# Row loads of two token blocks moved to GpSimd's queue in a fused attention and ReGLU training step

## The chip, the cores and the metric

The kernel runs on one core of a Trainium2 chip. A core has five engines that each work through their own list of instructions in order: TensorE (PE) for matrix products, VectorE (DVE), ScalarE (ACT), GpSimd (POOL) and SyncE (SP), which issues most data transfers. Transfers are issued into queues and carried out by the core's 16 DMA engines. The metric is the time of one execution on the device, in microseconds (us).

## The reference

A forward pass and its gradients by all weights and by `x`, in bf16. For 2048 tokens of width 512, a gate `g` mixes sliding-window attention (32 heads of 16, window 256) with a gated ReGLU feed-forward layer of 1376 columns:

```
x = A_x                                           # 2048 x 512
g = sigmoid((x * gate_w).sum(-1, keepdims=True))
q, k, v = heads(x @ wqkv)                         # 32 heads, 16 wide
scores = q k^T * 16**-0.5, kept where 0 <= i - j < 256
a = concat(softmax(scores) v) @ wo
gate = x @ W_gate; up = x @ W_up                  # 2048 x 1376
b = (gate * (gate > 0) * up) @ W_down
out = g * a + (1 - g) * b
grads = vjp(out)(grad_out)   # for x, wqkv, wo, W_gate, W_up, W_down, gate_w
```

There are eight outputs: `out` and seven gradients, out_7 being that of `gate_w` (512 values).

## The kernel before, in words

All work is written as small operations, each with the engines that may do it, an estimated duration, a rank, and the buffers it reads and writes. A planner (`Flow.run`) then plays through time when the kernel is built: at each moment it gives every idle engine the ready operation of lowest rank, and writes its instructions into that engine's list. So the order on each engine is fixed when the kernel runs, and comes from ranks, estimated durations and 27 seeds (`SEEDS`) that spread the ranks of dense products. An engine waits in order: an instruction that waits holds up all behind it.

SBUF is one big tile, `arena`, cut by hand into rings of buffers (`ring`), which may lie on top of one another where one group is used only after another. PSUM is eight banks that are handed out under caps by name (`CAP_S` for scores, `CAP_DP` and so on).

The stages overlap freely:

- Rows. `x` and `grad_out` are kept in SBUF as rows (`x_r`, `db_r`), in four blocks of 512 tokens. `load_first` (L726, L731) brings block 0 and the first weights through SP's and ACT's queues; `load_rows` (L717) brings blocks 1 to 3 through SP's queue, 512 KB each. `rows_to_T` (L772) turns each block on PE into `x_T` and `db_T`. The rows of `grad_out` are first scaled by 1 - g on DVE (L847), after `gates` has computed the gate of that block (L833 on PE, L839 to L841 on ACT).
- Projections. `proj` (through L673) makes q, k, v and the gradient on the heads for four chunks of 128 columns and stores them to DRAM (L808), from where the attention loads them again (L977 to L979). The weights of chunk 1 and of the first two feed-forward chunks come by POOL's queue (L699, L710); `proj_weights` regroups weights on POOL (L814, L817) and stores them (L820).
- Attention. 32 stages; in each, PE computes scores and their gradients (L1049), ACT the exponentials (L1090), POOL the mask (L1066), DVE a product (L1096), and PE the sums over keys or queries (L1112). The kinds of products are called row, col and den (dense) in the planner, which counts a cost for a switch between them.
- Feed-forward. `front` makes three products for each block and three elementwise products (L902, by DVE or POOL) and stores them (L905); `back` makes the weight gradients.
- The end. `early` makes the feed-forward part of tokens (L1401 on PE), `dw` the gradients of wqkv and wo (dWqkv rows are evicted into `dwst` and stored at L1329, dWo at L1337), and `final` and `whole` finish each token block: for twelve of the sixteen, two partial results (`b_d`, `dx_p`) are loaded again (L1489, L1490), POOL adds them (L1508, L1514), and SP stores the sums (L1510, L1516). `gate_sum` adds up `gate_w`'s gradient over the token blocks in a long sum on DVE (L1469), which is turned into two bf16 parts (L1472, L1473); `direct` (L1480) adds these parts and the last three token blocks by five small products, and the result is stored at L1563.

Where PE has nothing ready, the planner puts a dummy product into its list (L1568). A few lines of the constants and the loads:

```
gw_b = mc.tile([P, D], BF, name="gw_b")
gw_rep = mc.tile([P, DC, P], BF, name="gw_rep")
...
for sb in range(1, NSB):
    load_rows(x_r, x_d, sb)
    load_rows(db_r, go_d, sb)
```

## Time and profile before

| what | value |
|---|---|
| median of 3 runs | 814.55 us (811.65 to 815.1) |
| the profiled execution's own time | 811.5 us |
| its span, first to last instruction | 809.8 us |
| busy: PE, DVE, ACT, POOL | 785.8, 703.5, 595.6, 540.2 us |
| granted TensorE clock, mean | 1.000 |
| data moved | 152.18 MB, mean 188 GB/s |

The span is the part of the execution that the trace covers; 1.7 us lie around it. "Busy" of PE counts pipelined products, whose ends are modelled. Each instruction is named by the line of the kernel that wrote it; L673 and L1401 are helpers through which dense products of several stages pass, L651 and L653 the copies out of PSUM by ACT and DVE.

### The profile page before, as it was taken

To read this page: it belongs to the slowest core of one execution; us is meant where nothing else is said; L and a number is where in the kernel's file an instruction comes from. 1 tells how busy PE (TensorE), PEld (TensorE's weight loads), DVE (VectorE), ACT (ScalarE), POOL (GpSimd) and SP (SyncE) were. 2 spreads that over 40 slices of the span, in tenths; PEclk is the share of its full clock that TensorE was granted. 3 is DMA by queue.
4 is the path that set the end of the run, shared out by engine and by line. 5 is a ranking of instruction groups with operands and counts; after the bars stand their busy time and mean duration, and the time that the engine had idled before them with its cause. 6 is when DMAs were issued, how large, how long until landed. Compare 5 with 4: busy or idle time off the path is not lost.

```text
span 809.8 us, 24095 instructions
## 1 busy us (share of the span) xinstructions
PE 785.8 (97%) x8845; PEld 371.4 (46%) x8950; DVE 703.5 (87%) x1273; ACT 595.6 (74%) x1183; POOL 540.2 (67%) x950
## 2 busy tenths in 40 slices
PE   8899999999999999999999999999999999999998
PEld 5534444544445445454554545444434344344443
DVE  3589999999998999999999989999999999934664
ACT  4776988898888888888888887889888878413221
POOL 2488678787796979969888765666656666212235
PEclk9999999999999999999999999999999999999999
DMA  8699457577499997988998895963765547797996
GB/s 229 186 205 228 126 137 172 118 177 177 118 204 169 227 181 227 209 170 242 200 186 186 236 219 148 191 184 103 201 158 175 145 141 177 228 267 204 267 206 196
DMA packets 313009, 152.18 MB, mean 188 GB/s; under 512 B 203161, under 2 KB 303194, under 8 KB 312250
## 3 DMA queue, kind: packets, MB, share of 16 engines
q1 hardware_dynamic: 294706, 136.47, 70.3%
q10 hardware_dynamic: 17688, 12.72, 5.6%
q0 software_dynamic: 496, 1.44, 0.8%
q8 instruction: 70, 1.15, 0.6%
q14 instruction: 49, 0.40, 0.2%
HBM read 55.02 MB, written 55.74 MB: 137 GB/s over the span
## 4 chain that ended last, share of the span: by engine, by line
PE 81%; DVE 8%; issue 3%; DMA 3%; ACT 3%; POOL 1%; SPq 0%; POOLq 0%; DVEq 0%; ACTq 0%
PE banks L673 36%; PE banks L1401 18%; PE banks L1049 15%; PE banks L1112 9%; DVE arena L1096 3%; ACT arena L1090 2%; DMA arena<-b_d 1%; PE banks L772 1%; DVE arena L902 1%; PE banks L1147 1%; DMA out_dram<-arena 1%; DVE arena L897 1%; DMA arena<-HD_d 1%; DMA arena<-in_A_x_dram 0%; DVE arena L1145 0%
## 5 line engine op out<-in xcount | busy, mean ns | idle before, releaser
L1096 DVE TENSOR_TENSOR arena<-arena,banks 128x512 bf16<-128x512 bf16 (+1 forms) x740 | 456.2, 665 | 21.9 <-PE banks L1049 15.6
L1066 POOL TENSOR_SCALAR_AFFINE_SELECT arena<-arena 128x256 bf16<-128x256 bf16 (+1 forms) x752 | 354.3, 494 | 166.1 <-ACT arena L1090 145.4
L1090 ACT ACTIVATE arena<-banks 128x512 bf16<-128x512 f32 (+1 forms) x740 | 396.9, 588 | 87.1 <-PE banks L1049 68.0
L673 PE MATMUL banks<-arena 128*128 128x512 bf16 (+4 forms) x1915 | 382.9, 334 | 5.8 <-issue 2.6
L673 PEld LDWEIGHTS <-arena 128*128 128x128 bf16 (+1 forms) x1984 | 173.6, 98 | 154.7 <-issue 56.4
L1401 PE MATMUL banks<-arena 128*128 128x512 bf16 (+1 forms) x749 | 182.6, 380 | 3.4 <-issue 2.4
L1049 PE MATMUL banks<-arena 32*128 32x128 bf16 (+5 forms) x2944 | 157.2, 270 | 4.2 <-DVE arena L1096 1.8
L1049 PEld LDWEIGHTS <-arena 32*128 32x128 bf16 (+1 forms) x2944 | 48.8, 92 | 141.1 <-issue 137.9
L1401 PEld LDWEIGHTS <-arena 128*128 128x128 bf16 (+1 forms) x784 | 69.5, 98 | 89.6 <-issue 18.4
L902 POOL TENSOR_TENSOR arena<-arena 128x512 bf16<-128x512 bf16 (+1 forms) x84 | 97.9, 1169 | 16.0 <-DVE arena L897 15.0
L1112 PE MATMUL banks<-arena 128*32 128x128 bf16 (+5 forms) x2944 | 94.5, 271 | 1.0 <-DVE arena L1096 0.5
L651 ACT CAST arena<-banks 128x512 bf16<-128x512 f32 (+4 forms) x158 | 77.6, 502 | 22.8 <-PE banks L673 17.6
L1112 PEld LDWEIGHTS <-arena 128*32 128x32 bf16 (+1 forms) x2944 | 60.7, 95 | 32.4 <-issue 16.2
L1508 POOL TENSOR_TENSOR arena<-arena 128x512 bf16<-128x512 f32 x12 | 15.5, 1292 | 47.7 <-DMA arena<-b_d 25.5
L1143 POOL TENSOR_TENSOR arena<-arena 128x512 bf16<-128x512 f32 x32 | 37.0, 1155 | 9.4 <-issue 5.7
L1507 ACT ACTIVATE arena<-banks,g_all 128x512 f32<-128x512 f32 x12 | 8.0, 684 | 45.1 <-DVE arena L1498 16.5
L902 DVE TENSOR_TENSOR arena<-arena 128x512 bf16<-128x512 bf16 (+1 forms) x48 | 35.8, 752 | 0.2
L1514 POOL TENSOR_TENSOR arena<-arena 128x512 bf16<-128x512 f32 x12 | 16.1, 1341 | 21.5 <-DVE arena L1512 13.2
L897 DVE SCALAR_TENSOR_TENSOR arena<-arena,banks 128x512 bf16<-128x512 bf16 (+1 forms) x44 | 29.9, 679 | 0.2
L892 ACT ACTIVATE arena<-banks 128x512 bf16<-128x512 f32 (+1 forms) x41 | 25.0, 610 | 2.0 <-PE banks L673 1.5
L653 DVE CAST arena<-banks 128x512 bf16<-128x512 f32 (+2 forms) x42 | 23.8, 580 | 2.1 <-PE banks L673 0.9
L1498 DVE SCALAR_TENSOR_TENSOR arena<-banks,g_all,arena 128x512 bf16<-128x512 f32 x12 | 9.0, 746 | 18.2 <-ACT arena L1507 15.5
(96 smaller groups left out, 414.1 us busy)
## 6 DMA issues: line engine op xcount, KB each, us to landing
ffn_d<-arena SPq DMA_DIRECT2D x40, 384.0 KB
arena<-ffn_d SPq DMA_DIRECT2D x88, 128.0 KB
out_dram<-arena SPq DMA_DIRECT2D x66, 128.0 KB
arena<-HD_d ACTq DMA_DIRECT2D x26, 256.0 KB
KV_d<-arena SPq DMA_DIRECT2D x32, 128.0 KB
QD_d<-arena SPq DMA_DIRECT2D x32, 128.0 KB
arena<-KV_d SPq DMA_DIRECT2D x32, 128.0 KB
arena<-QD_d SPq DMA_DIRECT2D x32, 128.0 KB
```

Of the source, the lines that this page charges most:

```text
L651: nc.scalar.copy(out, in_)
L673: return lambda start, stop: nc.tensor.matmul(out_fn(), lhsT=lhs_fn(), rhs=rhs_fn(), start=start, stop=stop)
L892: nc.scalar.activation(q["rg"][:fs, :], gps[:fs, :], ACT.Relu)
L897: op({DVE: t_stt(W)}, lambda e, q=q, ups=ups: nc.vector.scalar_tensor_tensor(out=q["upm"][:fs, :], in0=q["rg"][:fs, :], scalar=0.0, in1=up ...
L902: op({POOL: t_pool(W, 2), DVE: DTT}, lambda e, q=q, k=k, a=a, b=b: EN[e].tensor_tensor(out=q["act"][:fs, k, :], in0=q[a][:fs, :], in1=q[b] ...
L1049: nc.tensor.matmul(bank, lhsT=lt[rs, ls], rhs=rt[rs, rsl], start=True, stop=True)
L1066: nc.gpsimd.affine_select(out=v.rearrange("p h (b k) -> p h b k", b=cnt), in_=v.rearrange("p h (b k) -> p h b k", b=cnt), compare_op=ALU.i ...
L1090: op({ACTE: t_act(w)}, lambda e, h=h: nc.scalar.activation(nxt.Pt[:, h, :w], nxt.S[h][:, :w], ACT.Exp), r=[nxt.S[h]], w=[(nxt.Pt, h)], rank=0)
L1096: op({DVE: t_dve(wc)}, lambda e, h=h: nc.vector.tensor_tensor(out=cur.Pd[:, h, :wc], in0=cur.Pt[:, h, :wc], in1=cur.dP[h][:, :wc], op=ALU. ...
L1112: nc.tensor.matmul(acc[32 * i:32 * i + wt.shape[1], q0:q0 + cnt * P], lhsT=wt, rhs=m[:, i % 2, col * P:(col + cnt) * P], start=(k == 0), s ...
L1143: op({POOL: t_pool(W, 2), DVE: t_dve(W)}, lambda e: EN[e].tensor_tensor(out=U[:], in0=ri[:], in1=qd[:], op=ALU.mult), r=[ri, qd], w=[U], r ...
L1401: nc.tensor.matmul(bank[:], lhsT=l_(), rhs=r_(), start=(lo + k == 0), stop=(lo + k == n - 1))
```

## The change

The rows of blocks 2 and 3 (the third and fourth) of `x` and `grad_out` are loaded by POOL's queue, with a lower rank number, so that they stand first there, ahead of the weights that POOL loads. SP keeps block 1. The planner gets a separate account of POOL's queue. The load of chunk 1's projection weights waits for the transposes of block 3 instead of block 1, and the regrouping of chunk 0's weights for the gradient rows of block 3 instead of the rows of block 2. The constants `gw_rep` and `gw_b` move from tiles of their own into the arena; `gw_b` is loaded only once the attention's buffers are free. `dwst` gets a second place in one area beside the one elsewhere, scores may hold four banks instead of three, the two products of the long gate sum come behind the last token blocks, and the seeds are new, so that the whole order is laid out anew.

```
-BACKLOG = 1500
+BACKLOG, SHARED = 1500, 120
-SEEDS = (31086, 16702, ...)
+SEEDS = (18831, 18193, ...)
...
-                    if dma_free > now + BACKLOG:
+                    if dma_free > now + BACKLOG and e != POOL:
                         cands = [o for o in cands if o.rank < 3 or not o.nbytes]
...
-                    if o.nbytes:
-                        dma_free = max(dma_free, now + took) + o.nbytes / 240
+                    if o.nbytes and e == POOL:
+                        pool_free = max(pool_free, now + took) + o.nbytes / SHARED
+                        post(pool_free + LATENCY[SP], "done", o)
+                    elif o.nbytes:
+                        begin, alone = max(dma_free, now + took), o.nbytes / 240
+                        dma_free = begin + alone + max(0, min(alone, (pool_free - begin) / 2))
...
-    DENSE, CAP_S, CAP_DP, CAP_MM, CAP_ACC = 4, 3, 4, 3, 2
+    DENSE, CAP_S, CAP_DP, CAP_MM, CAP_ACC = 4, 4, 4, 3, 2
+    ROWQ = 4
-    SB = 204 * KB
+    SB = 206 * KB
...
+    ring("gwr", 1, [P, DC, P])
-    ring("Pd", 9, [P, 2, W], at=rings["cs0"].lo, after=["cs0"])
+    ring("Pd", 9, [P, 2, W], at=rings["cs0"].lo, after=["cs0", "gwr"])
...
-    dwst_at = [(place_at["next"], proj_done), (A0, ["QDT"])]
-    place_at["next"] += 3 * P * 2
+    dwst_at = [(place_at["next"], proj_done), (place_at["next"] + 6 * P, proj_done), (A0, ["QDT"])]
+    place_at["next"] += 12 * P
...
+    ring("gwb", 1, [P, D], after=att)
...
-    def load_rows(dst, src_d, sb):
-        dma(lambda: nc.sync.dma_start(...), w=[(dst, sb)], nbytes=512 * KB, rank=3)
+    def load_rows(dst, src_d, sb, on=(SP,)):
+        dma(lambda q: q.dma_start(...), w=[(dst, sb)], nbytes=512 * KB, rank=2 if on == by_pool else 3, on=on)
...
-        load_rows(x_r, x_d, sb)
-        load_rows(db_r, go_d, sb)
+        load_rows(x_r, x_d, sb, by_pool if 2 * sb >= ROWQ else (SP,))
+        load_rows(db_r, go_d, sb, by_pool if 2 * sb + 1 >= ROWQ else (SP,))
...
-    proj_weights(0, [later[2]])
-    load_gate_rows([later[3]])
+    proj_weights(0, [later["db",3]])
...
-        load_proj(c, [later[1]] if c == 1 else ())
+        load_proj(c, [later[3]] if c == 1 else ())
...
-            for k in range(2):                     # in gate_sum, where the long sum ends
-                direct(lambda: ones_c[:], lambda k=k: gx2[:, k], [(gx2, k)])
...
+    for k in range(2):                             # behind all token blocks
+        direct(lambda: ones_c[:], lambda k=k: gx2[:, k], [(gx2, k)])
```

## The prediction

> **What bounds the kernel now.** I read the page's busy table first, then a table of stages, then the list of what TensorE (PE) waited for, then the first and the last microseconds one by one.
>
> ```profile
> span 809.8 us, 24095 instructions
> PE 785.8 (97%) x8845; PEld 371.4 (46%) x8950; DVE 703.5 (87%) x1273; ACT 595.6 (74%) x1183; POOL 540.2 (67%) x950
> ```
>
> PE is idle for 809.8 - 785.8 = 24.0 us in all. The table of stages has the length of each, the busy time of PE, its weight loads, DVE, ACT and POOL, then clock, DMA share and GB/s:
>
> ```profile
> 5.00:10.00 5.00, 4.78 (x35) 3.80 (x34) 0.85 (x2) 1.18 (x3) 0.47 (x1) 1.00 1.15 236
> 10.00:20.00 10.00, 9.91 (x96) 5.47 (x95) 6.03 (x14) 6.12 (x14) 0.86 (x1) 1.00 0.85 260
> 60.00:200.00 140.00, 137.07 (x1641) 63.08 (x1663) 135.09 (x231) 115.67 (x227) 109.91 (x187) 1.00 0.69 165
> 200.00:700.00 500.00, 489.85 (x6163) 230.74 (x6224) 474.79 (x844) 413.45 (x821) 363.27 (x668) 1.00 0.77 184
> 700.00:803.20 103.20, 101.71 (x557) 47.20 (x568) 57.59 (x125) 25.74 (x57) 32.00 (x29) 1.00 0.87 233
> 803.20:809.80 6.60, 3.01 (x14) 0.97 (x13) 0.00 (x0) 1.16 (x2) 3.06 (x3) 0.94 0.47 147
> ```
>
> From 60 to 700 PE is idle for 2.93 + 10.15 = 13.1 us in small pieces, and DVE is busy 135.09 of 140 and 474.79 of 500: two engines are nearly full, PE the fuller. From 700 to 803.2 only PE is full. The time is PE's queue of instructions, its start, and 6.6 us behind its last matrix product. In the instruction lists of the two builds PE has the same products before and after, save that the dummy ones (L1568) go from eight to four. The change can win or lose idle time, switches between kinds of products, and tail.
>
> **Part 1: rows by POOL's queue.** The four row loads that move, what PE waited for, and the DVE scalings of two row blocks with POOL's work beside the first:
>
> ```profile
> 13.71 0.47 SPq L717 DMA_DIRECT2D arena<-in_A_x_dram  x1
> 14.24 0.50 SPq L717 DMA_DIRECT2D arena<-in_grad_out_dram  x1
> 20.35 0.57 SPq L717 DMA_DIRECT2D arena<-in_A_x_dram  x1
> 27.56 0.45 SPq L717 DMA_DIRECT2D arena<-in_grad_out_dram  x1
> ```
> ```profile
> PE banks L772 <- DVE arena L847: 2.0, 2, 1.6
> PE banks L752 <- POOL ident masks.py:199: 1.6, 1, 1.6
> PE banks L772 <- DMA arena<-in_A_x_dram: 1.2, 1, 1.2
> PE banks L1049 <- ACT arena L1090: 0.4, 2, 0.2
> ```
> ```profile
> 19.14 1.15 POOL L902 TENSOR_TENSOR arena<-arena 128x512 bf16<-128x512 bf16 x1 [13.67 <-DVE arena L897]
> 19.19 3.23 DVE L847 TENSOR_SCALAR arena<-arena,omg_all 128x512 bf16<-128x512 bf16 x4 [0.21 <-ACT omg_all L841]
> 27.64 1.14 DVE L847 TENSOR_SCALAR arena<-arena,omg_all 128x512 bf16<-128x512 bf16 x4 [0.60 <-ACT omg_all L841]
> ```
>
> SP issues these four loads between 13.71 and 27.56, each behind stores that wait for computed blocks. But PE lost nothing to late rows there: its waits at the start are 1.6 us for the identity, 1.2 us for the first rows (both stay) and 2.0 us for the scaling L847, which took 3.23 us instead of 1.14 beside a POOL product. That product (L902) no longer lies there: in the new lists all four scalings and all row transposes come before POOL's first L902. So I take the 2.0 us as won. At the other end, POOL's two weight regroupings (L814, L817) still lie near the later scalings and could stretch one as L902 did: then nothing is won.
>
> The risk is that the rows come late by the new queue. In the new order PE transposes block 2 (the third) before block 1, after only eight projection products. What POOL's queue does so early is seen with the weights that it loads now; the number behind KB is us from issue to landing:
>
> ```profile
> 3.03 0.95 POOL L710 DMA_DIRECT2D arena<-in_B_W_gate_dram  x1
> 3.98 0.76 POOL L710 DMA_DIRECT2D arena<-in_B_W_up_dram  x1
> 4.72 0.75 POOL L699 DMA_DIRECT2D arena<-in_A_wqkv_dram  x1
> ```
> ```profile
> arena<-in_B_W_gate_dram POOLq DMA_DIRECT2D x1, 128.0 KB, 5.6
> arena<-in_B_W_up_dram POOLq DMA_DIRECT2D x1, 128.0 KB, 5.2
> arena<-in_A_wqkv_dram POOLq DMA_DIRECT2D x1, 128.0 KB, 6.2
> ```
>
> They land at 3.03 + 5.6 = 8.6, 9.2 and 4.72 + 6.2 = 10.9: 1.15 us for each further 128 KB, in pieces of 256 bytes. Rows come in pieces of 1 KB, and the stage 10 to 20, which moves mostly such pieces, gets 260 / 0.85 = 306 GB/s from a full set of engines against 236 / 1.15 = 205 in the stage 5 to 10: a factor of 1.5. So 0.77 us for each 128 KB: block 2 of x lands at 8.6 + 3 x 0.77 = 10.9, its gradient rows at 14.0, block 3 of x at 17.1, its gradient rows at 20.1. When PE needs them comes from its order and these rows of the chain of waits:
>
> ```profile
> 10.62 0.11 PE banks L685
> ...
> 24.35 0.89 PE banks L772 x16
> 26.54 0.38 PE banks L833 x16
> 31.75 0.32 PE banks L1049 x4
> ...
> 45.69 1.40 PE banks L673 x6
> ...
> 712.53 10.75 PE banks L1401 x49
> ```
>
> Before, the gate's little transpose (L685) ended at 10.7; two more products at 1.40 / 6 = 0.233 us make 11.1, when block 2 is wanted. From there to block 3 PE has 64 transposes (3.6 us), 16 products (3.7 us) and two groups of L833 (0.8 us): 19.2. Both are met, the first by 0.2 us only. The gain of part 1 is -2.0 us; the bounds are -2.0 and the rival of late rows below.
>
> A rule of the Trainium skill speaks against the part. Its page DMA: Bandwidth & Descriptors, section Issuing engines are not separate DMA queues, says that loads issued from different engines share the same DMA engines and interleave, so that a second issuer saves only issue time. By that rule the rows get no bandwidth, and part 1 is worth nothing but order. The stage 5 to 10, with its DMA share at 1.15, agrees; the issue times up to 27.56 show that issue order was the limit here, though not PE's.
>
> **Part 2: PE's order.** The row loads let the planner lay out everything anew. Counted in the lists, PE switches between its three kinds of products (dense, scores, columns) 816 times instead of 827. Six dense products between scores take 1.40 us; in a long run they take 6 x 10.75 / 49 = 1.32: 0.08 us a switch, and eleven fewer give -0.9 us (bounds -0.9 and 0). Two of the four dummy products now lie in the attention's end instead of behind everything, where they were free: 2 x 0.22 = +0.4 us. These are rows of the page for what moves between engines:
>
> ```profile
> L902 DVE TENSOR_TENSOR arena<-arena 128x512 bf16<-128x512 bf16 (+1 forms) x48 | 35.8, 752 | 0.2
> L653 DVE CAST arena<-banks 128x512 bf16<-128x512 f32 (+2 forms) x42 | 23.8, 580 | 2.1 <-PE banks L673 0.9
> ```
>
> Seven of 48 front products (L902) leave DVE for POOL, 7 x 0.752 = -5.3 us; copies come to DVE from ACT, net of smaller ones that leave it some eight of 512 columns, 8 x 0.580 = +4.6 us. Of this net -0.7 us of DVE I take -0.4 us on the path, since DVE is 95% busy (bounds -0.7 and +0.7). A fourth bank for scores is worth at most the 0.4 us that score products waited for ACT; I take 0.
>
> **Part 3: the tail.** These rows show who is last:
>
> ```profile
> 803.14 0.59 PE L1480 MATMUL banks<-arena,ones_c 128*1 128x512 bf16 x2
> 803.77 1.26 POOL L1508 TENSOR_TENSOR arena<-arena 128x512 bf16<-128x512 f32 x1
> 804.42 0.57 ACT L651 CAST arena<-banks 1x512 bf16<-1x512 f32 x1 [0.58 <-PE banks L1480]
> 805.00 1.26 POOL L1514 TENSOR_TENSOR arena<-arena 128x512 bf16<-128x512 f32 x1
> 806.28 0.33 SPq L1516 DMA_DIRECT2D out_dram<-arena  x1
> 807.18 0.27 SPq L1563 DMA_DIRECT2D out_dram<-arena  x1
> ```
>
> The gate's row is in SBUF at 804.99, but its store (L1563) goes out at 807.18, because SP stands in order behind the store of POOL's last sum (806.28). Alone it would go at 805.05: 2.1 us. In the new order ACT has done its last copy for a token block (L1511, L1507) before it evicts any of the last three dWqkv groups, where before it did two behind the second; so POOL's sums should end earlier against PE. I take -1.5 us. Against it, the gate's two conversions (L1472, L1473) move from DVE to POOL, ahead of its last four pairs; if POOL stays last, two operations at 1.26 make +2.5. The bounds are -2.1 and +2.5. Adding the long sum last costs PE nothing: the same five products stand at the end.
>
> **Edits at nothing.** `gw_rep` in the arena: its last reader precedes the first `Pd` in PE's order, and `gw_b`, now loaded only after the attention, stands in SP's list ahead of the first final store; DVE first read it at 726.96:
>
> ```profile
> 726.96 0.75 DVE L1512 SCALAR_TENSOR_TENSOR arena<-gw_b,arena 128x512 f32<-128x512 bf16 x1 [0.91 <-ACT arena L1511]
> ```
>
> If it came late, DVE and POOL would wait, with PE's hundred microseconds of queued products as cover. The third place for dWqkv rows serves a stage where PE had 101.71 of 103.20 busy: nothing to win.
>
> **The sum.** -2.0 - 0.9 + 0.4 - 0.4 - 1.5 = -4.4 us. The profiled execution took 811.5 us (its span and 1.7 around it), so a like one would take 807.1. The median of the runs is 814.55, 3 us above it; from the median the forecast is 810.2 us. About 0.5%, 4.1 us, is what a measurement of this kernel can tell from no change, so the forecast lies just beyond it.
>
> **Rivals.**
> *The attention starts late and is not caught up (slower).* Before the first score products PE now has 34 more dense products, 16 more transposes and one more L833 group: 7.9 + 0.9 + 0.4 = 9.2 us; with the 2.0 us won, the first scores move from 31.75 to about 39. Behind the last column product stand 435 products in both lists, so the attention has to make up 7.2 us, mostly before its first third is through. For it: DVE had only 4.9 us idle from 60 to 200. Against it: DVE's early idle time (3.97 us from 10 to 20 alone) takes up work that was in the attention. It decides where DVE is above 99% busy in that stretch; then the end moves by up to 7.2 - 0.9 + 0.4 - 0.4 = +6.3, taken as 5: 819.5.
> *Rows come late (slower).* At 1.5 times the weights' pace, 1.73 us for each 128 KB, since SP's own rows share the engines, block 2 lands at 13.8 (2.7 late) and block 3 at 27.6 against 21.9 (5.7 late): +8.4 instead of -2.0, in all +6.0: 820.6. It decides from a landing of block 2 after 11.1.
> *No change.* The skill's rule above would give this: rows were not late, the stall at L847 returns at another scaling, and POOL stays last at the tail: -0.9 + 0.4 - 0.4 = -0.9: 813.7.
> *More than forecast.* The new order also halves the 13.1 us of small idle pieces: -4.4 - 6.5, taken as -9: 805.6. Nothing in the lists shows it.
>
> **How the numbers follow.** Forecast 0.42 (806 to 812.5 by its bounds; 0.34 of it faster, 0.08 the same); attention late 0.17 (0.14 slower, 0.03 the same); rows late 0.09 (0.08 slower, 0.01 the same); no change 0.25 (0.22 the same, 0.03 slower); more 0.07, all faster. So faster 0.41, same 0.34, slower 0.25. The range from 803 to 819.5 leaves out a little of the last case and the upper part of the two slow ones, under 0.2 in all.
>
> **What would show it.** Right: no wait of PE on a row load after the first, L847 at 1.14 us four times, first scores near 39, last column product not later than 712, and the gate's store within 2 us of its copy. Wrong: PE waiting on a POOL load between 11 and 20 us; DVE full and PE idle for over 5 us from 60 to 200; POOL's sums last at the end by more than before.

## The result, and the profile after

The changed kernel takes 825.35 us (822.15 to 831.72), the kernel before beside it 814.25: a ratio of 1.0141, 95% interval 1.0107 to 1.0174. The change makes the kernel 11 us slower; the forecast was 810.2 us, range 803 to 819.5. The profiled execution took 824.03 us. (Ratios here and below leave out executions more than 1.5% above the fastest of their kernel, two of e5's nine and two of e11's four; medians do not.)

The page's head and the table of stages, columns as before the change; the two stages with odd borders are cut to where the granted clock is low:

```profile
span 822.3 us, 24210 instructions
PE 799.9 (97%) x8946; PEld 374.3 (46%) x8946; DVE 709.4 (86%) x1271; ACT 592.5 (72%) x1177; POOL 551.2 (67%) x962
```
```profile
5.00:10.00 5.00, 5.00 (x36) 3.78 (x34) 0.85 (x2) 1.17 (x2) 4.24 (x6) 1.00 1.08 331
10.00:20.00 10.00, 6.48 (x81) 4.06 (x79) 6.20 (x16) 5.12 (x12) 4.25 (x6) 1.00 1.06 277
20.30:27.10 6.80, 5.24 (x38) 4.14 (x39) 1.38 (x2) 2.77 (x3) 1.93 (x3) 0.50 0.56 184
60.00:200.00 140.00, 137.46 (x1560) 62.44 (x1559) 133.34 (x227) 110.14 (x215) 109.95 (x185) 1.00 0.71 165
200.00:700.00 500.00, 496.05 (x6292) 231.38 (x6292) 477.46 (x840) 418.50 (x836) 375.73 (x688) 1.00 0.79 182
784.90:788.20 3.30, 3.30 (x10) 1.15 (x8) 0.00 (x0) 0.00 (x0) 0.82 (x1) 0.50 0.60 202
```

From 60 to 700 little has changed (a part of the larger idle time before is missing records, see the section on the prediction). What is new is 3.5 us of idle PE between 10 and 20, where it had been busy 9.91 of 10, and two stretches at half the clock, at 20 and at 785 us. What PE waited for (total, times, longest) names two loads:

```profile
PE banks L778 <- DMA arena<-in_A_x_dram: 6.2, 2, 5.0
PE banks L1407 <- DMA arena<-HD_d: 2.3, 2, 2.1
PE banks L1054 <- DVE arena L658: 1.8, 1, 1.8
```

The first is block 1 of x. The timeline of SP shows its issue, the timeline of POOL its loads (here the releaser of each POOL load is the landing of a row load), and PE's shows the wait, the first score products and the end of the last column products:

```profile
4.60 1.86 SPq L748 DMA_TRANSPOSE arena<-in_A_wo_dram  x1
6.51 0.68 SPq L723 DMA_DIRECT2D arena<-in_A_x_dram  x1
```
```profile
3.04 0.97 POOL L723 DMA_DIRECT2D arena<-in_A_x_dram  x1
...
8.45 0.78 POOL L716 DMA_DIRECT2D arena<-in_B_W_up_dram  x1
10.94 0.75 POOL L705 DMA_DIRECT2D arena<-in_A_wqkv_dram  x1 [1.70 <-DMA arena<-in_A_x_dram]
12.48 0.75 POOL L705 DMA_DIRECT2D arena<-in_A_wqkv_dram  x1 [0.79 <-DMA arena<-in_grad_out_dram]
14.08 0.75 POOL L705 DMA_DIRECT2D arena<-in_A_wqkv_dram  x1 [0.85 <-DMA arena<-in_A_x_dram]
```
```profile
21.86 1.03 PE L778 MATMUL banks<-ident,arena 128*128 128x128 bf16 x8 [5.02 <-DMA arena<-in_A_x_dram]
...
45.77 0.40 PE L1054 MATMUL banks<-arena 16*128 16x384 bf16 x8
...
719.69 0.72 PE L1117 MATMUL banks<-arena 128*32 128x128 bf16 x24
```

POOL's blocks land at 10.9, 12.5 and 14.1, as early as they are wanted. Block 1, issued by SP at 6.51, lands at 21.8, 15.3 us later, and PE stands for 5.02 us. In between the two queues (packets, MB, share of 16 engines, from 9 to 16 us) move this:

```profile
q0 software_dynamic: 564, 1.91, 95.1%
q1 hardware_dynamic: 543, 0.13, 12.9%
```

As many packets each, but POOL's (q0) hold 4096 bytes where those of wo's transpose on SP (q1), ahead of block 1 in its order, hold 256 (a few of 4 bytes aside): 15 bytes to one. The 0.13 MB are just the transpose's 128 KB, so of block 1 hardly anything has moved by 16. The first scores start at 45.77 instead of 31.75, the last column product ends at 719.69 + 0.72 = 720.4 instead of 712.4, as the timeline before has it:

```profile
711.96 0.41 PE L1112 MATMUL banks<-arena 128*16 128x128 bf16 x2 [0.52 <-DVE arena L1096]
```

So 8 us are lost by the end of the attention and 4.5 of the 12.5 in the tail. There the chain of waits has the second load, and the timeline the copy of the gate's row and SP's last stores:

```profile
776.03 0.47 ACTq L1385
...
776.59 7.91 DMA arena<-HD_d
784.50 0.04 issue
784.54 1.61 PE banks L1407 x4
```
```profile
816.79 0.57 ACT L656 CAST arena<-banks 1x512 bf16<-1x512 f32 x1 [0.63 <-PE banks L1484]
818.62 0.41 SPq L1520 DMA_DIRECT2D out_dram<-arena  x1
819.11 0.54 SPq L1335 DMA_DIRECT2D out_dram<-arena  x1
819.75 0.43 SPq L1569 DMA_DIRECT2D out_dram<-arena  x1
```

### The profile page after: what moved, and what is told of

It is laid out like the page before. It is cut to its first block, busy times and chain, and to the rows that moved or that the text cites. A ratio compares the mean times of both kernels' runs of the same rounds, so it can differ in the third digit from the quotient of the medians.

```text
span 822.3 us, 24210 instructions
## 1 busy us (share of the span) xinstructions
PE 799.9 (97%) x8946; PEld 374.3 (46%) x8946; DVE 709.4 (86%) x1271; ACT 592.5 (72%) x1177; POOL 551.2 (67%) x962
## 3 DMA queue, kind: packets, MB, share of 16 engines
q8 instruction: 70, 1.15, 0.6%
## 4 chain that ended last, share of the span: by engine, by line
PE 77%; DVE 9%; DMA 7%; issue 2%; ACT 1%; POOL 1%; SPq 1%; POOLq 0%; DVEq 0%; ACTq 0%
PE banks L678 35%; PE banks L1407 18%; PE banks L1054 14%; PE banks L1117 9%; DVE arena L1101 4%; DMA arena<-in_A_x_dram 2%; DMA arena<-HD_d 1%; DMA out_dram<-arena 1%; PE banks L1152 1%; DVE arena L1475 1%; PE banks L778 1%; DVE arena L1516 1%; DVE arena L1320 1%; ACT arena L1095 1%; DMA arena<-KV_d 1%
## 5 line engine op out<-in xcount | busy, mean ns | idle before, releaser
L1101 DVE TENSOR_TENSOR arena<-arena,banks 128x512 bf16<-128x512 bf16 (+1 forms) x740 | 456.6, 665 | 19.6 <-PE banks L1054 16.2
L1095 ACT ACTIVATE arena<-banks 128x512 bf16<-128x512 f32 (+1 forms) x740 | 395.9, 589 | 84.2 <-PE banks L1054 66.7
L678 PE MATMUL banks<-arena 128*128 128x512 bf16 (+4 forms) x2000 | 393.5, 336 | 1.0 <-DVE arena L1101 0.4
L1407 PE MATMUL banks<-arena 128*128 128x512 bf16 (+1 forms) x784 | 189.7, 383 | 2.4 <-DMA arena<-HD_d 2.3
L907 POOL TENSOR_TENSOR arena<-arena 128x512 bf16<-128x512 bf16 (+1 forms) x91 | 106.0, 1169 | 5.2 <-ACT arena L656 2.6
L656 ACT CAST arena<-banks 128x512 bf16<-128x512 f32 (+5 forms) x157 | 74.4, 488 | 29.0 <-PE banks L678 24.9
L1512 POOL TENSOR_TENSOR arena<-arena 128x512 bf16<-128x512 f32 x12 | 16.2, 1354 | 46.0 <-DMA arena<-b_d 17.5
L1148 POOL TENSOR_TENSOR arena<-arena 128x512 bf16<-128x512 f32 x31 | 36.0, 1160 | 6.1 <-issue 5.2
L658 DVE CAST arena<-banks 128x512 bf16<-128x512 f32 (+3 forms) x43 | 27.2, 639 | 7.9 <-PE banks L678 5.8
L1515 ACT COPY arena<-banks 128x512 f32<-128x512 f32 x12 | 6.9, 586 | 37.2 <-POOL arena L1518 24.7
L656 ACT COPY arena<-banks 128x512 f32<-128x512 f32 (+3 forms) x24 | 17.2, 716 | 16.4 <-PE banks L778 10.2
L1146 DVE SCALAR_TENSOR_TENSOR arena<-banks,vec,arena 128x512 bf16<-128x512 f32 x32 | 23.8, 744 | 1.7 <-ACT arena L1145 1.4
```

The source lines that it names most:

```text
L656: nc.scalar.copy(out, in_)
L658: EN[e].tensor_copy(out, in_)
L678: return lambda start, stop: nc.tensor.matmul(out_fn(), lhsT=lhs_fn(), rhs=rhs_fn(), start=start, stop=stop)
L907: op({POOL: t_pool(W, 2), DVE: DTT}, lambda e, q=q, k=k, a=a, b=b: EN[e].tensor_tensor(out=q["act"][:fs, k, :], in0=q[a][:fs, :], in1=q[b] ...
L1095: op({ACTE: t_act(w)}, lambda e, h=h: nc.scalar.activation(nxt.Pt[:, h, :w], nxt.S[h][:, :w], ACT.Exp), r=[nxt.S[h]], w=[(nxt.Pt, h)], rank=0)
L1101: op({DVE: t_dve(wc)}, lambda e, h=h: nc.vector.tensor_tensor(out=cur.Pd[:, h, :wc], in0=cur.Pt[:, h, :wc], in1=cur.dP[h][:, :wc], op=ALU. ...
```

## The experiments

Two questions: what makes the front's wait, and is that wait the loss, or is it the order of instructions that was planned around it? Where nothing else is said the planned order is kept and only where or when a transfer is issued is edited (the orders of e7 and e8 differ from the changed kernel's behind 794 and 623 us). The letters of theories and rivals are those of the expectations.

| kernel | us, median | ratio to before (95%) |
|---|---|---|
| changed | 825.35 | 1.0141 (1.0107 to 1.0174) |
| e1 wo behind block 1 | 821.31 | 1.0077 (1.0027 to 1.0126) |
| e2 rows on ScalarE's queue | 824.92 | 1.0138 (1.0083 to 1.0192) |
| e3 small transposes in the tail (leaves out a part of dWqkv) | 821.46 | 1.0088 (1.0058 to 1.0117) |
| e4 old order, rows first on POOL | 816.25 | 1.0029 (1.0014 to 1.0044) |
| e5 wait filled with products | 819.82 | 1.0074 (1.0044 to 1.0104) |
| e6 new order, rows on SP | 823.91 | 1.0133 (1.0098 to 1.0168) |
| e7 long sum put back | 824.53 | 1.0132 (1.0095 to 1.0169) |
| e8 other tie-breaks in the tail | 822.27 | 1.0114 (1.0056 to 1.0172) |
| e10 x first | 824.17 | 1.0148 (1.0099 to 1.0198) |
| e11 tail by POOL | 832.40 | 1.0149 (1.0121 to 1.0178) |
| e12 both | 824.91 | 1.0143 (1.0122 to 1.0163) |
| e13 rows planned on SP | 820.51 | 1.0071 (1.0042 to 1.0100) |
| e14 rows part alone on the kernel before | 837.51 | 1.0265 (1.0236 to 1.0294) |
| e15 changed, old tie-breaks | 838.59 | 1.0289 (1.0266 to 1.0313) |
| e16 rows on SP, old tie-breaks | 822.03 | 1.0089 (1.0057 to 1.0122) |
| e17 rows on SP, new draw | 818.85 | 1.0063 (1.0046 to 1.0081) |
| e18 rows on POOL, one price | 821.80 | 1.0091 (1.0077 to 1.0104) |

Runs of one changed kernel scatter more than those of the kernel before (e1: 814.15 to 824.65), so steps of 2 to 4 us among them are weak evidence.

### Which bytes come late: e1, e2, e6, e10

e1 moves wo's transpose behind block 1:

```diff
-        dma(lambda: nc.sync.dma_start_transpose(out=woT[:], in_=A_wo[0:P, :]), w=[woT], nbytes=128 * KB, rank=2.9, turn=True)
+        dma(lambda: None, w=[woT], nbytes=128 * KB, rank=2.9, turn=True)
...
+            if dst is x_r and sb == 1:
+                nc.sync.dma_start_transpose(out=wsets["pw", 0][1][:], in_=A_wo[0:P, :])
```

> The changed kernel, with the transposed load of wo's first chunk issued on SP's queue behind block 1 of x instead of ahead of it; all else, the planned order too, as in the changed kernel. Theory A (on SP's queue, which works in order, the 256-byte packets of this transpose are served in turn with the 4096-byte packets of GpSimd's queue, so the queue stalls and block 1 of x lands at 21.8 us): block 1 of x lands near 13 to 15 us, TensorE's waits of 5.0 us on it go, the clock is not halved from 20 us on, and the time falls by 6 to 8 us against the changed kernel, to some 817 to 819 us. Rival B (the 2 MB more that are asked for by 15 us simply fill the DMA engines, whatever the packets and their order): block 1 still lands after 19 us and the time falls by less than 2 us. Rival C (the loss is the new planned order, not the loads): the waits may go, yet the time stays within 2 us of the changed kernel.

The wait shrinks to 3.04 us and stays: block 1 lands at 18.4. The queues from 9 to 14 us:

```profile
q0 software_dynamic: 365, 1.36, 79.2%
q1 hardware_dynamic: 368, 0.38, 24.9%
```

SP's packets are now 1024 bytes, and still get one turn in two: 0.38 MB of 1.74. Theory A in its first form, the small packets, is half of it; block 1 landed some 4 us later than it said. The time fell by 4 to 5 us instead of 6 to 8.

The other three edit load_rows (`load` is its `dma_start` on a queue): e2, then e6, then e10, which has e1's edit as well.

```diff
-        dma(lambda q: q.dma_start(dst[:, 4 * sb:4 * sb + 4, :],
+        dma(lambda q: (nc.scalar if on == by_pool else q).dma_start(dst[:, 4 * sb:4 * sb + 4, :],
```
```diff
+            if sb == 1 and dst is x_r:
+                for d, s, k in ((x_r, x_d, 1), (x_r, x_d, 2), (db_r, go_d, 1), (x_r, x_d, 3), (db_r, go_d, 2), (db_r, go_d, 3)):
+                    load(nc.sync, d, s, k)
```
```diff
+            if dst is x_r:
+                load(q, x_r, x_d, sb)
+                if sb == 1:
+                    nc.sync.dma_start_transpose(out=wsets["pw", 0][1][:], in_=A_wo[0:P, :])
+                    load(nc.sync, db_r, go_d, 2)
+            elif sb == 1:
+                for k in (1, 3):
+                    load(nc.sync, db_r, go_d, k)
```

> The changed kernel, with the four row loads of blocks 2 and 3 issued on ScalarE's queue in place of GpSimd's, at the same places of the plan. Theory A (it is the 4096-byte packets of GpSimd's queue against the 256-byte ones of the transpose): with ScalarE's queue in 1024-byte packets SP's queue gets some four times the share it had, block 1 of x lands before 16 us, TensorE waits on it under 1 us, and the time falls by 5 to 8 us, to 817 to 820 us. Rival B (sheer bytes): block 1 of x lands after 19 us as in the changed kernel, and the time stays within 2 us of it. Rival C (the order): waits gone, time within 2 us of the changed kernel.

> The changed kernel in its own planned order, with all six later row loads on SP's queue: x 1, x 2, grad_out 1, x 3, grad_out 2, grad_out 3, issued at the place of x 1; GpSimd issues none. With the run of the old order with rows first on GpSimd's queue (816.25 us) and the two kernels this makes all four pairs of order and queue. Theory A (GpSimd's queue starves SP's): block 1 of x lands before 15 us, no wait of TensorE over 1.5 us ahead of 60 us, no halved clock there, and the time falls by 5 to 8 us, to 817 to 820 us. Rival C (the new order loses by itself): the time stays within 2 us of the changed kernel even without the wait. Rival B (bytes): the last blocks land after 25 us, and TensorE waits some 5 us on these instead.

> The changed kernel in its own planned order, with the early loads in the order in which they are needed: GpSimd issues only blocks 2 and 3 of x; on SP block 1 of x goes ahead of wo's transpose, grad_out 2 behind it, grad_out 1 and 3 where the changed kernel issues grad_out 1. Nothing is taken away, 1 MB of grad_out that is needed only behind 30 us is asked for later. Theory J (the new order needs block 1 of x, and then all of x, earlier than the DMA engines bring them once 4 MB are asked for together; which bytes come first decides, not which queue): block 1 of x lands before 17 us, no wait of TensorE over 1.5 us between 5 and 60 us, no halved clock there, first score product near 38 us, and 6 to 9 us less, 816 to 819 us. Rival C (the order loses anyway): front repaired, yet the time stays over 821 us, since waits come up elsewhere. Rival B (bytes alone): another load takes the place, wait over 3 us.

PE's longest front wait in e2, e6 and e10, one timeline line each:

```profile
21.67 0.51 PE L778 MATMUL banks<-ident,arena 128*128 128x128 bf16 x6 [2.47 <-DMA arena<-in_A_x_dram]
```
```profile
16.85 1.89 PE L785 MATMUL banks<-ident,arena 128*128 128x128 bf16 x16 [5.41 <-DMA arena<-in_A_x_dram]
```
```profile
18.97 1.03 PE L790 MATMUL banks<-ident,arena 128*128 128x128 bf16 x8 [3.81 <-DMA arena<-in_A_x_dram]
```

None of the four places for the same bytes serves this order. By ScalarE in 1024-byte packets block 1 lands at 21.7, as late as by POOL, though PE stands only 2.47 us there, having waited 1.95 us for ScalarE before. All on SP, block 2 is late instead, at 16.9. With x ahead of everything, block 1 lands at 19.0. The times stay at 821 to 825 us. The gains of 5 to 9 us of theories A and J did not come (e1's 4 to 5 us are the most): rival B and rival C were nearer.

### The same loads under the old order: e4

```diff
+                while fc == 0 and by_pool_first:
+                    by_pool_first.pop(0)(nc.gpsimd)
                 q.dma_start(t_[:, :, :fs], src[:, f0:f0 + fs].rearrange("(c p) f -> p c f", p=P))
...
+        if sb > 1:
+            by_pool_first.append(load)
+        dma(lambda: load(nc.sync) if sb == 1 else None,
             w=[(dst, sb)], nbytes=512 * KB, rank=3)
```

> The kernel before, in its own planned order and with everything else of it, but the four row loads of blocks 2 and 3 are issued first on GpSimd's queue. Theory A (GpSimd's row loads starve SP's queue, on which block 1 of x stands behind wo's transpose): block 1 of x lands after 18 us, TensorE waits 5 to 8 us on it, and the time is 6 to 11 us above the kernel before, some 820 to 825 us. Rival C (the loss belongs to the new order): no more than 2 us above the kernel before, or below it.

The wait list:

```profile
PE banks L780 <- DMA arena<-in_A_x_dram: 2.0, 2, 1.2
PE banks L780 <- DVE arena L855: 2.0, 2, 1.6
PE banks L673 <- DMA arena<-in_B_W_gate_dram: 1.6, 1, 1.6
```

Block 1 lands at 17.8, late by the same queue, and the cost is 1.8 us (816.25 against 814.48): this order wants it late and has other products meanwhile. Theory A's 6 to 11 us are refuted for this order. The early loads cost 2 us under the old order; the new order with them costs 11.

### The clock: e5

```diff
+                for _ in range(22 if src is x_r and (sb, h) == (1, 0) else 0):
+                    fl.fill(pt.got[0])
```

> The changed kernel, with 22 dummy products of 128x512 on TensorE right ahead of the transposes of block 1 of x, for which it waits 5.0 us in the changed kernel (some 4.7 us of work at 0.21 us each, so that the wait is filled but hardly shortened or lengthened). Theory A2 (the wait costs twice: its own 5 us, and then a halved clock for 6.83 us, some 3.4 us of TensorE's work): no halved stretch near 20 us, the first score product 3 to 4 us earlier than at 45.77 us, and the time lower by 3 to 4 us, some 821 to 822 us. Rival F (the halved clock costs little, since the products of that stretch wait for loads anyway): first score product within 1 us of 45.8 us, time within 1.5 us of the changed kernel.

PE's timeline and the stage that had been at half clock:

```profile
15.72 4.91 PE L1576 MATMUL banks<-arena,ident 128*128 128x512 bf16 x22
21.26 0.62 PE L780 MATMUL banks<-ident,arena 128*128 128x128 bf16 x8 [0.63 <-DMA arena<-in_A_x_dram]
```
```profile
20.30:27.10 6.80, 6.17 (x93) 4.50 (x92) 2.24 (x4) 4.83 (x8) 1.92 (x3) 1.00 0.78 208
```

`fill` is the kernel's dummy product. The data comes no earlier, but the clock is full, the first scores start at 42.65 instead of 45.77, and the ratio falls from 1.0141 to 1.0074, by some 5 us where 3 to 4 were expected; the two intervals just do not overlap. This wait was paid twice. (The profiled execution took 830.95 us, with a wait of 5.5 us for HD_d in the tail; its front alone is read here.)

### The tail: e3, e7, e8, e11, e12

e3, e7, e8 (the last three tie-breaking numbers) and e11; e12 has the edits of e10 and e11.

```diff
-                out=RW[:, 4 * sb:4 * sb + 4, :], in_=HD_d[c, :, :, sb * W:(sb + 1) * W].rearrange("k p s -> (k p) s")),
+                out=RW[:, 4 * sb:4 * sb + 4, 0:P], in_=HD_d[c, 0, :, sb * W:(sb + 1) * W]) if c == 3 and sb > 1 else
...
```
```diff
             op({POOL: t_pool(W, 2), DVE: DTT}, lambda e: EN[e].tensor_tensor(
                 out=gx2[:, 1], in0=gx[:], in1=gx2[:, 0], op=ALU.subtract), r=[gx, (gx2, 0)], w=[(gx2, 1)], rank=1.5)
+            for k in range(2):
+                direct(lambda: ones_c[:], lambda k=k: gx2[:, k], [(gx2, k)])
...
-    for k in range(2):
-        direct(lambda: ones_c[:], lambda k=k: gx2[:, k], [(gx2, k)])
```
```diff
-    47222, 14709, 1189, 8775, 604, 55191, 102, 33368, 54056, 30834, 41096,
+    47222, 14709, 1189, 8775, 604, 55191, 102, 33368, 40183, 31304, 15322,
```
```diff
-            dma(lambda q, c=c: q.dma_start(qk[:, 4 * c:4 * c + 4, :], HD_d[c, :, :, gsl].rearrange("k p s -> p k s")),
+            dma(lambda q, c=c: (nc.gpsimd if g == 7 and c else q).dma_start(qk[:, 4 * c:4 * c + 4, :], HD_d[c, :, :, gsl].rearrange("k p s -> p k s")),
```

> The changed kernel, with the last two DMA transposes of the third chunk of dQKV at a quarter of their size (that leaves out a part of dWqkv's last rows). Of the 12.5 us by which the last store comes later, some 4.5 arise behind the last column product. Theory D (these transposes, issued at 773.9 and 776.5 us, hold up the last loads of HD_d, for which TensorE waits 2.1 us and after which the clock is halved for 3.4 us): the wait and the halved stretch go, the time falls by 3 to 4.5 us, to 821 to 822 us. Rival E (the loads are late because ScalarE issues them late, at 776 to 778 us, behind its waits on GpSimd and VectorE): the wait stays over 1.5 us and the time within 1.5 us of the changed kernel.

> The changed kernel, with the two products of the gate's long sum added where the kernel before adds them, not last; the order differs from the changed kernel's only behind some 794 us. Theory G (the long sum put last is worth nothing, since GpSimd's sums and the stores behind them end last in both): the time within 1.5 us of the changed kernel. My prediction's term: put last, the sum lets the gate row's store go with the others and saves 1.5 us, so that undoing it costs 1.5 us, some 826 to 827 us. Rival: it is this that lengthens the tail, and undoing it saves 3 to 4 us.

> The changed kernel, with the tie-breaking numbers of the plan's last three blocks taken from the kernel before; the order on TensorE differs from some 623 us on and not ahead of it. Theory H (the some 4.4 us that the changed kernel takes longer from the last column product to its end, 102.19 us against 97.84 us, are a matter of which order the plan happens to draw there, with waits of over 1.5 us that halve the clock): this tail differs from 102.2 us by 2 us or more, the waits for HD_d fall or grow with it, and the time moves by as much. Rival I (what the change does to the tail, the long sum last and the places of the constants, lengthens it whatever the order): the tail stays within 1.5 us of 102.2 us.

> The changed kernel, with three of the last four HD_d loads before the waiting products (the ones that ScalarE issues at 775.6 to 778 us, behind its waits) on GpSimd's queue, whose engine stands idle from 773 us. Theory E (the loads are late because ScalarE issues them late): they are issued from 773 us on, TensorE's waits of 0.3 and 2.1 us on them go, the clock is not halved at 785 us, and the time falls by 3 to 4 us, to some 821 to 822 us. Rival D (the loads are slow because the DMA engines are full with the two transposes): the wait stays over 1.5 us, time within 1.5 us of the changed kernel.

> The changed kernel with both repairs: the early loads in the order of need, and the three late HD_d loads on GpSimd's queue. If the loss is made of the front's wait with its halved clock and of the tail's wait with its own (theory J with E), the gains add up to 9 to 13 us, some 812 to 816 us, no more than the kernel before within 2 us; if the new order loses by itself (rival C), it stays over 820 us.

e3: the longest wait for HD_d falls from 2.05 to 1.52 us only, the clock is still halved behind it, while the time is the one that D gave; between D and E, undecided. e7: 824.53, as changed, so no gain by the place of the long sum shows; but its tail also got eight more dummy products, some 1.8 us, and a term of 1.5 us would be lost in the scatter. e8: its tail from the start of the last column product is 102.3 us, as in the changed kernel (102.1), which speaks for rival I, but that was read in the longest of its runs (818.63 to 829.26); it settles little. e11 did not gain. POOL's timeline and PE's wait, from an execution of 837.64 us (two others took 824.81 and 827.17):

```profile
777.30 2.32 POOL L1385 DMA_DIRECT2D arena<-HD_d  x3
```
```profile
PE banks L1407 <- DMA arena<-HD_d: 15.8, 3, 9.8
```

GpSimd issues them no earlier (its own two sums came later in this run), and on a third queue they landed later. Probably that is because b_d's and dx_p's loads, which stood behind them on ScalarE's queue, now run beside them; no run separates this. Since they were not issued earlier, E was not really tried, and D, contention, is no more than the nearer; e12 has the front of e10 and this tail, and gains nothing. Why the HD_d loads come late in the tail stays open.

### Plan or loads: e13 to e18

All six are planned anew. e13 sets ROWQ to 8; e14 is the kernel before with the change's lines on ROWQ, load_rows, BACKLOG, SHARED and pool_free alone; e15 is the changed kernel with the SEEDS of the kernel before, e16 the same with ROWQ at 8, e17 the same with other SEEDS. e18 takes the second pipe out of the plan's prices:

```diff
-    ROWQ = 4
+    ROWQ = 8
```
```diff
-                    if o.nbytes and e == POOL:
-                        pool_free = max(pool_free, now + took) + o.nbytes / SHARED
-                        post(pool_free + LATENCY[SP], "done", o)
-                    elif o.nbytes:
-                        begin, alone = max(dma_free, now + took), o.nbytes / 240
-                        dma_free = begin + alone + max(0, min(alone, (pool_free - begin) / 2))
+                    if o.nbytes:
+                        dma_free = max(dma_free, now + took) + o.nbytes / 240
```

> The changed kernel with every row load planned on SP's queue (the number from which rows go by GpSimd is set from 4 to 8), planned anew with the changed kernel's tie-breaking numbers; the long sum last, the constants in the arena and all else stay. Theory K (the plan counts on blocks 2 and 3 by GpSimd at 120 bytes per ns beside SP's loads, which then run at no less than half their rate; the loads don't come like that, and the order that is built on it loses): without these loads no wait of TensorE over 1.7 us ahead of 60 us, no halved clock there, and 813 to 818 us. Rival L (the loss comes from the other parts or from the draw of tie-breaks): the time stays above 820 us.

> The kernel before with one part of the change alone: the rows of blocks 2 and 3 go by GpSimd's queue, with the plan's new pricing of that queue; its own tie-breaking numbers, constants and sums stay, and it is planned anew. Theory K: a wait of TensorE over 2 us on block 1 of x ahead of 30 us, with a halved clock, and 818 to 826 us. Rival L: the time stays within 3 us of the kernel before, 811 to 817 us.

> The changed kernel planned anew with the kernel before's tie-breaking numbers, all else as changed. Theory K: the wait on block 1 of x is there in this draw too, over 2 us with a halved clock, and the time is 819 to 828 us. Rival L (the draw decides): 812 to 818 us, without that wait.

> The changed kernel with every row load planned on SP's queue and the kernel before's tie-breaking numbers. Theory K: like the other kernel with rows planned on SP, no wait over 1.7 us ahead of 60 us, and 812 to 817 us; if its tail is as short as before's, the long sum last could show here as up to 1.5 us less than 814 us. Rival L: above 820 us.

> The changed kernel with every row load planned on SP's queue, as in two runs before this (820.5 and 822.0 us), and with tie-breaking numbers drawn anew, so that the plan's own end comes out earliest among some 900 draws. Theory K: no wait of TensorE over 1.7 us ahead of 60 us. If the 6 to 7 us by which those two runs lie above the kernel before are the draw, this one comes down to 808 to 815 us, about the kernel before or under it; if the other parts of the change (the long sum last, the constants in the arena, the third place) cost by themselves, it stays at 818 us or more.

> The changed kernel, rows of blocks 2 and 3 still issued first on GpSimd's queue, but the plan prices every transfer, GpSimd's too, on one common pipe of 240 bytes per ns, as the kernel before does; planned anew with the changed kernel's tie-breaking numbers. Theory K (the loss is the order that is built on transfers that do not come as priced): the plan asks for the blocks later, no wait of TensorE over 2 us ahead of 60 us, and 816 to 822 us, as with the rows planned on SP (820.5 us). Rival M (the early loads by GpSimd cost by themselves, whatever the plan expects): a wait over 3 us and a halved clock stay, 824 us or more.

Rows by GpSimd against rows by SP: 825.35 against 820.51 with the new tie-breaks, 838.59 against 822.03 with the old, 837.51 against 815.14 on the kernel before. The row part loses in all three pairs, 5, 17 and 22 us. The first row of the wait list in e14 and e15, then what is left for x in e13:

```profile
PE banks L777 <- DMA arena<-in_A_x_dram: 7.1, 2, 5.9
```
```profile
PE banks L778 <- DMA arena<-in_A_x_dram: 6.2, 2, 5.0
```
```profile
PE banks L778 <- DMA arena<-in_A_x_dram: 1.1, 1, 1.1
```

The wait comes with the row part in each draw and goes with it, as theory K said; the times do not follow it. e14 and e15 came out 10 to 12 us above K's ranges, e13 and e16 2.5 and 5 us above, where rival L had put them. The wait and the halved clock behind it (6.83 us in both) can make at most 5.9 + 3.4 us of e14's 22 and 5.0 + 3.4 of the 23 by which e15 lies above the kernel before. A part of the rest is in the plans: e14 and e15 hold 25 and 49 dummy products of some 0.22 us, the changed kernel four, the kernel before eight, and a dummy product stands where the plan had nothing ready for PE. e14 has two further waits of 3.0 and 3.1 us. e15's busy row:

```profile
PE 811.8 (97%) x8991; PEld 378.7 (45%) x8991; DVE 704.5 (84%) x1261; ACT 595.9 (71%) x1188; POOL 551.8 (66%) x961
```

e18 then separates the loads from their price: GpSimd issues the same four loads first, and the queues from 9 to 14 us share the engines as before, but the plan no longer believes in a pipe of POOL's own:

```profile
q0 software_dynamic: 450, 1.59, 94.4%
q1 hardware_dynamic: 431, 0.11, 11.8%
```
```profile
PE banks L774 <- DMA arena<-in_A_x_dram: 1.2, 1, 1.2
```

The wait is gone (1.2 us is the first rows' alone), the first scores start at 31.72, as before the change, and the time is 821.8 us. So the loads by GpSimd need not cause the wait; the order that the plan built on their price did. That is 3.5 of the 11 us, in one draw.

Open remains the rest: 818.85 to 822.03 us without the wait on block 1, 4 to 7 us above the kernel before, in four plans (e13, e16, e17, e18). e13, e16 and e18 hold 18, 21 and 23 dummy products, of which 10, 15 and 15 stand ahead of the last real product (before: none), and their clock is at half for 3.41, 6.83 and 6.83 us between 270 and 590 us. e17 has three dummy products, but waits of 2.9, 2.7 and 2.2 us and a mean clock of 0.990. The wait of 2.7 us, ahead of the first scores, is against K's word that none over 1.7 would come ahead of 60 us, and the clock is at half from 31.61 to 41.85 us with it:

```profile
PE banks L1054 <- DMA arena<-QD_d: 2.7, 1, 2.7
```

So much of this rest is seen in the plans, as dummy products and new waits, and not in the row loads. Whether a better draw would reach the kernel before, or the constants' places cost by themselves, isn't settled: the constants alone under the old order weren't tried, since moving them plans everything anew. No version beat the kernel before.

## Why the prediction was wrong

**The step that failed is "Both are met, the first by 0.2 us only"** in part 1: it asked only for the loads that move, and put at nothing what they do to block 1 of x, which stays. For POOL's loads it was right: block 2 was put at 10.9 and landed at 10.94, its gradient rows at 14.0 and 12.5, block 3 at 17.1 and 14.1. The first agreement was in part luck, since the pace behind it, 3.1 us for each 512 KB, was twice the 1.5 us measured. Its factor of 1.5, from pieces of 256 bytes to 1 KB, had no ground in the trace either: before, POOL's queue moved 1.44 MB in 496 packets, 2.9 KB each. Block 1 of x stays on SP, and the new order wants it at 16.8; it landed at 21.8. I had the pieces: the new order with block 1 right behind block 2, the transpose ahead of it, engines already full in the stage 5 to 10 (1.15). The term -2.0 should have been -1.6 + 5.0 and the halved clock behind it. (Of the 2.0 us for the scaling 1.6 were won: one of the four still took 2.24 us, not 1.14, but PE waits only 0.4 us behind it.)

**The rule I weighed.** I read "Issuing engines are not separate DMA queues" as worth nothing but order. The Trainium skill, page DMA: Bandwidth & Descriptors, section Queues, rings and completion order, adds that each engine takes turns between the rows that have work, packet by packet. The trace agrees (564 packets to 543). By that, a second queue with larger packets takes bandwidth from the first: not zero, but a loss. Packet size alone does not decide it: with 1024-byte packets on ScalarE's queue (e2) block 1 landed no earlier.

**Rivals.** "The attention starts late and is not caught up" was right in kind. I put the first scores at 39, they came at 45.77, and the difference of 6.8 us is about the wait of 5.0 us and the halved clock behind it. Of the 14.0 us by which they are late, 8 were left at the last column product. That it would end at 819.5 was too mild. "Rows come late" had the right cause and the wrong block: it priced POOL's.

**The idle time.** I took 13.1 us of idle PE from 60 to 700, of 24.0 in all. But that trace has 8845 products beside 8950 weight loads, so 105 products are missing from its busy time. e4 has the same order and a record for each:

```profile
60.00:200.00 140.00, 139.18 (x1653) 63.40 (x1651) 135.83 (x232) 116.07 (x227) 109.73 (x184) 1.00 0.69 166
200.00:700.00 500.00, 496.00 (x6233) 230.69 (x6232) 475.14 (x843) 413.01 (x821) 364.57 (x669) 1.00 0.78 183
```

There the idle time is 0.8 + 4.0 = 4.8 us. The case "More than forecast", which halved it, had little to win.

**Part 2** was small, as forecast, and smaller. e4's PE row has 795.7 us busy of 811.9, at full clock but for the very end. The changed kernel has 799.9, of which 5.2 and 3.3 us lie in the two halved stretches and took twice their time, 4.3 us; 795.6 is left. So PE's busy time fell by 0.1 us, and the dummy products, four instead of eight, make more than that (1.2 us instead of 1.9): no gain by fewer switches shows. What DVE's lighter load did would lie in the idle time and is not separated. Idle time is 822.3 - 799.9 = 22.4 against 811.9 - 795.7 = 16.2. The 10.4 us between the two spans are 6.2 of idle time, 4.3 of clock and -0.1.

```profile
PE 795.7 (98%) x8950; PEld 371.3 (46%) x8950; DVE 704.1 (87%) x1273; ACT 596.0 (73%) x1183; POOL 543.9 (67%) x954
```

**Part 3** failed in size and sign. POOL's sums stay last, the gate's store goes out at 819.75, 2.4 us behind its copy, as 2.2 before; the -1.5 did not come. What came was not on my list: 2.3 us of waits for HD_d and the clock at half for 3.41 us behind them, 1.7 us, which make 4.0 of the 4.5 us that were lost behind the last column product. Why these loads came late is not settled (e3, e11).

**Range.** It held no case where a wait costs a second time by the clock, and its slow cases had the price of one block's lateness.

## What to carry to other kernels

When a transfer is moved to another queue, list what stays on the old one and ask when that lands: on full engines queues share turns, not bytes. When a planner or a reordering builds on new landing times, price them on one common pipe, and look for the first instruction that would stand if they were late. And a TensorE wait of some 2 us or more may count twice, once for itself and once for the clock behind it; the one that was filled with dummy products here counted once.

## What the runs showed of the hardware

While two queues had work, they took turns packet by packet, whatever the size: 564 to 543, 365 to 368 and 450 to 431 packets in three kernels, with 4096 bytes against 256 or 1024.

The granted clock went to 0.50 for 3.41 us or whole multiples of it (6.83, 10.24), and its changes lie on a fixed grid in each trace. In the changed kernel they come at 20.28, 27.11, 784.87 and 788.28 us: 2, 224 and 225 steps of 3.413 us behind the first. What counts, as far as these traces tell, is how long PE is idle within one step. A wait of 1.77 us (e1, from 175.66) lay within one step, and the next was halved; so did the 2.05 us (changed, from 782.49), and of the waits of 3.04 us (e1) and 5.02 us (changed) 2.6 us and a whole step of 3.4 lay within one. A wait of 2.47 us (e2, from 19.20) and one of 1.81 (changed, from 179.26) crossed a border of the grid, with 1.35 and 1.44 us in one step, and went without. In the 15 traces that lack no products, all 29 steps with 1.87 us or more of idle PE were followed by a halved one; from 0.76 to 1.83 us both occur. e1's stage behind the 1.77 us, and e2's stage around its 2.47:

```profile
178.40:181.70 3.30, 3.30 (x10) 1.37 (x11) 3.30 (x7) 2.81 (x6) 2.08 (x4) 0.50 0.72 166
```
```profile
17.00:24.00 7.00, 4.53 (x57) 3.46 (x56) 4.74 (x14) 3.93 (x8) 1.98 (x3) 1.00 0.96 314
```

The Trainium skill's page TensorE: Matmul & The Clock Gate, section HAM oscillation — how this bites in real kernels, gives as the abstract rule to avoid idle gaps of more than some 3.4 us; the runs here halve the clock from gaps of about half that.
